# Mask factors by GpSimd, first loads in another order, and half of a layer's weights converted after attention

## The chip, the cores and the metric

The kernel runs on one core of one Trainium2 chip. The metric is device time in microseconds (us) of one execution. The core's engines are PE (matrix multiply; PEld is its weight load), DVE (vector), ACT (activations), POOL (GpSimd) and SP, which here issues every DMA. Each engine works through its own queue in order. A change of under 0.2%, about 2 us, can hardly be told from no change.

## What is computed

The inputs are the heads' `q`, `k`, `v` (4 sequences, 8 heads, 576 positions, 64 channels) and two layers' weights. Attention's mask is block-causal over blocks of 64 positions. The kernel receives every weight as 64-bit floats, which it reads as pairs of 32-bit words.

```python
scores = scale * q @ k.T            # (4, 8, 576, 576), masked: block_i >= block_j
attn   = softmax(scores)
x = (attn @ v) -> (2304, 512)
h = x @ w_in;  x = max(0.01*h, h) @ w_out                # first layer, 512 -> 2048 -> 512
h = x @ w_in2; g = P(h) / (Q(h) + 1e-6); out = g @ w_out2  # second layer, same shape
```

## The kernel before

**Stages.** The program runs 32 heads one after another (loop over `heads`). Behind the first batch of eight heads, the first layer of a finished batch is laid into the gaps: `moe1` is a generator that yields after each matmul, and `fill(n)` takes n of them between a head's steps. After the last head the rest of the first layer runs alone (32 calls of `fill(24)`, then `drain`): 512 tokens of the last batch, then 256 left-over tokens. Then `moe2`, the second layer, runs to the end. Matmuls take a number as a high and a low part (`wh`, `wl`), three products for one.

**Conversion.** `convert` is a generator that turns raw 64-bit weights into the two parts, block by block, two `yield`s (halves) for a block of 128 x 512 numbers. For each block SP loads 512 KB of raw words into a tile `cs` (three buffers, `load_block`). In the first half ACT scales the high words (line 165), and POOL (first nine blocks, line 169) or ACT (line 171) the low words. In the second half DVE joins them into `cl` (line 180), ACT rounds them to the high part (line 183), and POOL subtracts to get the low part (line 184). The first 32 blocks are the first layer's; their high part stays in SBUF and the low part is written to HBM (`w1l`). The last 32 blocks are the second layer's, two for each of 16 groups `f`; both parts are written to HBM (`w2h`, `w2l`, 256 KB each) and loaded again: groups 0 to 7 after attention, in the 32 `fill(24)` steps, into tiles `w2a` and into the space of the tiles `xh`, `xl` (`w2_in_x`), and groups 8 to 15 at the start of `moe2`.

**Order.** `pace` calls `cv` so that after head n `due[n]` halves are done: 65 up to head 14 (all of the first layer's blocks and one half) and 63 more over heads 15 to 31. Only SP's queue stands in the order of the code; a scheduler sets the other engines' orders from their dependences. Each DMA on SP's queue also waits for the landing of the one eight before it.

**Heads.** The first eight heads (`n < NSF`) multiply plain 32-bit tiles `fq`, `fk`: rows 0 to 63 hold q and k, rows 64 to 127 hold mask factors (`mask`: a memset, line 208, and an affine select, line 210, of 64 rows each, on POOL). There are four pairs of such tiles. POOL fills two pairs, and four DMAs copy the second pair's factors into pairs three and four (line 662). ACT scales q for each head (`a1`, line 243). In a head, scores go into PSUM tiles `T` of which four exist (`a2_part`, line 289 or 295), DVE takes maxima (line 301), ACT exponentiates (line 307), and the rows are divided by their sums (`a2_norm`, line 317, on DVE for the first eight heads and on POOL after). PE transposes the result (line 344), ACT and DVE move it out of PSUM (lines 327, 329, 334, 337), PE multiplies by v (lines 372, 376) and ACT and DVE take that out (lines 383 to 385, 389, 390, 393, 394; the last 64 positions go to HBM as `xld`).

Of the kernel before, what the change touches and what calls it, by code (L numbers as in the profile page):

```python
# [25 lines left out]
def attention_moe_moe_kernel(  # L26
# [13 lines left out]
    nc = tc.nc  # L40
# [78 lines left out]

    W1L = dram.tile([2 * NF, P, KD, P], F32, name="w1l")  # L120
    W2H = dram.tile([NF, P, 2 * KD, P], F32, name="w2h")
    W2L = dram.tile([NF, P, 2 * KD, P], F32, name="w2l")
# [4 lines left out]
    for g, c in enumerate(CUTS):  # L127
# [3 lines left out]
        for d in range(KD):  # L131
            src = w1_out[512 * g:512 * (g + 1), 2 * d * P:2 * (d + 1) * P].rearrange("(r p) w -> p r w", p=P)
            blocks.append((src, (w1o[:, 4 * g:4 * g + 4, d * P:(d + 1) * P], W1L[NF + 4 * g + d]), True))
    for f in range(NF):
        src = w2_in[:, 2 * f * P:2 * (f + 1) * P].rearrange("(r p) w -> p r w", p=P)
        blocks.append((src, (W2H[f, :, 0:KD, :], W2L[f, :, 0:KD, :]), False))
        src = w2_out[f * P:(f + 1) * P, :].rearrange("p (r w) -> p r w", r=KD)
        blocks.append((src, (W2H[f, :, KD:2 * KD, :], W2L[f, :, KD:2 * KD, :]), False))
    stage = {}
# [4 lines left out]
    def load_block(i):  # L144
        if i < len(blocks):
            stage[i] = cp.tile([P, 512, 2], I32, tag="cs", name="cs", bufs=3)
            nc.sync.dma_start(out=stage[i].rearrange("p (r n) w -> p r (n w)", r=KD), in_=blocks[i][0])

    split = []

# [6 lines left out]
    def convert():  # L157
        load_block(0)
        load_block(1)
        for i in range(len(blocks) + 1):  # L160
# [11 lines left out]
            if i > 0:  # L172
                s = stage.pop(i - 1)
                _, (dh, dl), kept = blocks[i - 1]
                hi, lo = s[:, :, 1], s[:, :, 0]
                f = cp.tile([P, KD, P], F32, tag="cl", name="cl", bufs=3)
                wh = dh if kept else cp.tile([P, KD, P], F32R, tag="ch", name="ch", bufs=2)
                hi, lo = (x.rearrange("p (r c) -> p r c", c=P) for x in (hi, lo))
                yield
                nc.vector.scalar_tensor_tensor(  # L180
                    f.bitcast(I32), hi, 3, lo, ALU.logical_shift_left, ALU.bitwise_or
                )
                nc.scalar.copy(wh, f)
                nc.gpsimd.tensor_tensor(f.bitcast(F32R), f, wh.bitcast(F32), ALU.subtract)
                write_block()
                split.append(((dh, wh.bitcast(F32)), (dl, f))[kept:])
                yield
        write_block()

    ndone = [0]  # L190
    conv = convert()

    def cv(n):
        for _ in range(n):
            next(conv, None)

    def cv_to(i):
        while ndone[0] < i:
            next(conv, None)

# [295 lines left out]
    def drain():  # L496
        while filler[0] is not None:
            fill(1000)


    chunks = [(NT1 * c, NT1) for c in range(B)] + [(B * NT1, B * NL)]
    W2 = {}

# [147 lines left out]
    with tc.manual_schedule(engines={mybir.EngineType.SP}):  # L651
        nc.scalar.preload_act_table_set("natural_log_exp_and_others")
        for n in range(4):
            load_qk(n)
        load_v(0)
        load_v(1)
        for c, (val, base) in enumerate(((1.0, 0), (NEG, 64))):
            mask(plain[0][c], val, base)
        for c, (val, base) in enumerate(((1.0, 0), (NEG, 64))):
            mask(plain[1][c], val, base)  # L660
            for j in (2, 3):
                nc.sync.dma_start(out=plain[j][c][D:P, :], in_=plain[1][c][D:P, :])
        make_identity(nc, ident)
        for e in range(2):
            for i in range(5):
                nc.gpsimd.memset(PB[e][i][:, KEYS[i]:], 0.0)
        nc.vector.memset(cq, 1.0 + EPS_Q)

        heads = [(b, h) for b in range(B) for h in range(H)]

        due = [0, 2, 4, 5, 9, 11, 13, 17, 22, 29, 36, 42, 48, 59, 65] + [65 + 63 * n // 17 for n in range(1, 18)]
        ncv = [0]
# [25 lines left out]
        for n, (b, h) in enumerate(heads):  # L698
# [8 lines left out]
            for step, f in zip(steps, fills):  # L707
                if step == "1" and n + 1 < NHD:
                    a1(n + 1)
                elif step == "v":  # L710
                    if n >= WHOLE:
                        a1v(n)
                    if n < WHOLE and odd and 0 < p:
                        load_v(p + 1)
# [38 lines left out]
        tiles = [w2_tiles(w2a, f) for f in range(NA)] + [w2_in_x(pair, f) for f in range(2)]  # L753
        loads = chain(*(load_w2_by_part(f, *t) for f, t in enumerate(tiles)))
        for i in range(32):
# [5 lines left out]
            elif i == 14:  # L761
                nc.scalar.copy(X[B][0], X[B][1].bitcast(F32))
                nc.vector.tensor_tensor(X[B][1], X[B][1].bitcast(F32), X[B][0].bitcast(F32), ALU.subtract)
                nc.vector.tensor_scalar(coef[:, 0:4], cab[:, 0:4], -1.0, None, ALU.mult)
                nc.scalar.activation(coef[:, 4:6], cab[:, 4:6], AF.Abs)
            elif i < 14:
                next(loads, None)
            elif i == 15:
                pair = x_tiles()
                loads = chain(*(load_w2_by_part(NA + 2 + f, *w2_in_x(pair, f)) for f in range(2)))  # L770
                loads = chain(loads, load_x2(0))
                filler[0] = moe1(B) if filler[0] is None else chain(filler[0], moe1(B))
            elif i % 2:
                next(loads, None)
        drain()
        store_x2()
# [43 lines left out]
```

## Time and profile before

| | us |
|---|---|
| median of 3 runs | 1042.35 (1041.92 to 1043.25) |
| the profiled execution | 1041.77 |
| its span, first to last instruction | 1040.0 |
| PE busy | 996.7 |
| DVE, ACT, POOL busy | 736.7, 668.9, 271.5 |

The profile is of one execution. The span is what the trace covers; 1.8 us of that execution lie outside it. PE's time is given as busy from a matmul's start to its modelled end, so matmuls in a row overlap, and what counts is where PE is idle.

### The profile page before, as it was taken

What the parts mean: (1) busy time and instruction counts of PE and PEld (TensorE: products, weight loads), DVE (VectorE), ACT (ScalarE), POOL (GpSimd) and SP (SyncE); (2) the same over time, 40 slices, a digit from 0 to 9 for tenths busy, and PEclk for the clock granted to TensorE, in tenths of its full rate; (3) what the DMA queues carried; (4) which work ended last, traced back from release to release, by engine and by line L of the source; (5) the groups of instructions that cost most, each with busy time, mean ns of one, the idle gap of its engine ahead of it and who ended that gap; (6) DMA issues with size and microseconds to landing.
All of it is one profiled execution on the core that took longest, in us unless ns stands there. A gap on an engine that the chain in (4) does not pass through costs nothing.

```text
span 1040.0 us, 14689 instructions
## 1 busy us (share of the span) xinstructions
PE 996.7 (96%) x4968; PEld 822.8 (79%) x4968; DVE 736.7 (71%) x1270; ACT 668.9 (64%) x1371; POOL 271.5 (26%) x325
## 2 busy tenths in 40 slices
PE   6989988999999989999999999999999999999998
PEld 4657776787888877888888899888888888888886
DVE  5897777676777767765322224999888888888885
ACT  5778878667776767675311324876766766676675
POOL 3366647464655544533100101000000000000000
PEclk9999999999999999999999999999999999999999
DMA  7467869468668676663755697702102000110010
GB/s 202 135 189 260 284 204 296 157 206 268 223 183 234 203 257 207 202 184 121 233 183 191 206 302 278 288 1 82 41 1 81 21 21 1 40 41 1 1 41 21
DMA packets 101995, 158.32 MB, mean 152 GB/s; under 512 B 11168, under 2 KB 48032, under 8 KB 101920
## 3 DMA queue, kind: packets, MB, share of 16 engines
q1 hardware_dynamic: 101920, 157.39, 47.4%
q8 instruction: 39, 0.64, 0.3%
q14 instruction: 36, 0.29, 0.1%
HBM read 116.92 MB, written 39.85 MB: 151 GB/s over the span
## 4 chain that ended last, share of the span: by engine, by line
PE 62%; DMA 11%; ACT 9%; DVE 8%; issue 4%; POOL 3%; SPq 2%; ACTq 0%; DVEq 0%; POOLq 0%
PE M L461 20%; PE h L563 19%; PE o L617 19%; DMA cs<-in_moe_w_in_dram 3%; ACT PB L307 3%; DVE nm L301 2%; DMA cs<-in_moe_w_out_dram 2%; DMA xld<-vr 2%; DVE cl L180 1%; ACT cs L165 1%; PE T L344 1%; ACT pTh L329 1%; PE T L376 1%; DMA qk<-in_k_dram 1%; DMA qk<-in_q_dram 1%
## 5 line engine op out<-in xcount | busy, mean ns | idle before, releaser
L461 PE MATMUL M<-gh,w1o 128*128 128x512 f32 (+1 forms) x320 | 121.3, 379 | 6.7 <-DVE vr L390 3.5
L461 PE MATMUL M<-gl,w1o 128*128 128x512 f32 (+1 forms) x320 | 120.7, 377 | 0.0
L461 PE MATMUL M<-gh,wl 128*128 128x512 f32 (+1 forms) x320 | 120.3, 376 | 0.0
L575 ACT ACTIVATE ea<-h,coef 128x512 f32<-128x512 f32 (+1 forms) x80 | 51.6, 645 | 92.7 <-PE h L563 92.7
L307 ACT ACTIVATE PB<-T,nm 128x448 f32<-128x448 f32 (+4 forms) x160 | 82.9, 524 | 36.1 <-DVE nm L301 35.0
L469 ACT ACTIVATE gh<-M 128x512 fp32r<-128x512 f32 (+1 forms) x80 | 44.5, 556 | 89.8 <-PE M L461 89.8
L471 DVE TENSOR_TENSOR gl<-M,gh 128x512 fp32r<-128x512 f32 (+1 forms) x80 | 50.6, 633 | 70.5 <-ACT M L470 70.5
L563 PE MATMUL h<-x2h,w2l 128*128 128x512 f32 (+1 forms) x240 | 88.9, 370 | 0.0
L563 PE MATMUL h<-x2h,w2h 128*128 128x512 f32 (+1 forms) x240 | 88.9, 370 | 0.0
L563 PE MATMUL h<-x2l,w2h 128*128 128x512 f32 (+1 forms) x240 | 88.8, 370 | 0.0
L617 PE MATMUL o<-w2h,g2l 128*128 128x512 f32 x216 | 84.7, 392 | 0.0
L617 PE MATMUL o<-w2h,g2h 128*128 128x512 f32 x216 | 84.7, 392 | 0.0
L317 POOL TENSOR_SCALAR PB<-PB,sm 128x448 f32<-128x448 f32 (+4 forms) x120 | 71.1, 612 | 51.9 <-DVE sm L314 51.9
L617 PE MATMUL o<-w2l,g2h 128*128 128x512 f32 x216 | 84.6, 391 | 0.0
L578 DVE SCALAR_TENSOR_TENSOR ea<-eh,coef,ea 128x512 f32<-128x512 f32 (+1 forms) x80 | 55.7, 696 | 34.9 <-ACT eh L576 34.5
L344 PE MATMUL T<-ident,PB 128*128 128x128 f32 x480 | 66.8, 278 | 11.5 <-ACT PB L307 4.8
L301 DVE TENSOR_REDUCE nm<-T 128x1 f32<-128x448 f32 (+4 forms) x160 | 71.3, 478 | 8.6 <-PE T L289 7.9
L461 PE MATMUL M<-xh,w1i 128*128 128x512 f32 x256 | 74.6, 401 | 2.8 <-DVE vr L390 2.5
L461 PEld LDWEIGHTS M<-gh,w1o 128*128 128x128 f32 x320 | 60.5, 189 | 19.0 <-ACT PB L307 3.9
L344 PEld LDWEIGHTS T<-ident,PB 128*128 128x128 f32 x480 | 54.6, 142 | 26.0 <-ACT PB L307 8.1
L180 DVE SCALAR_TENSOR_TENSOR cl<-cs 128x512 int32<-128x512 int32 x64 | 57.0, 892 | 23.0 <-ACT cs L171 9.6
L461 PE MATMUL M<-xh,wl 128*128 128x512 f32 x256 | 73.1, 401 | 0.0
(122 smaller groups left out, 2528.4 us busy)
## 6 DMA issues: line engine op xcount, KB each, us to landing
wl<-w1l SPq DMA_DIRECT2D x160, 256.0 KB, 3.3
cs<-in_moe_w_in_dram SPq DMA_DIRECT2D x32, 512.0 KB, 5.5
cs<-in_moe_w_out_dram SPq DMA_DIRECT2D x32, 512.0 KB, 5.7
w1l<-cl SPq DMA_DIRECT2D x32, 256.0 KB, 4.8
w2h<-ch SPq DMA_DIRECT2D x32, 256.0 KB, 4.1
w2l<-cl SPq DMA_DIRECT2D x32, 256.0 KB, 4.3
w2h<-w2h SPq DMA_DIRECT2D x12, 512.0 KB, 7.0
w2l<-w2l SPq DMA_DIRECT2D x12, 512.0 KB, 7.7
```

The source lines that it names most:

```text
L180: nc.vector.scalar_tensor_tensor(f.bitcast(I32), hi, 3, lo, ALU.logical_shift_left, ALU.bitwise_or)
L301: nc.vector.tensor_reduce(nm[:, i:i + 1], sc, axis=AX.X, op=ALU.max, negate=True)
L307: nc.scalar.activation(PB[e][i][:, 0:ln], sc, AF.Exp, scale=SCALE if n == 0 else 1.0, bias=nm[:, i:i + 1], accum_out=sm[:, i:i + 1])
L317: (nc.vector if n < WHOLE else nc.gpsimd).tensor_scalar(PB[e][i][:, 0:ln], PB[e][i][:, 0:ln], sm[:, i:i + 1], 1.0, ALU.mult, ALU.mult)
L344: nc.tensor.transpose(T[:, c:c + P], PB[e][i][:, kt * P:(kt + 1) * P], ident)
L461: nc.tensor.matmul(T, lhsT=w[:, kk, :], rhs=A[kk][lo], start=(m == 0), stop=(m == 11))
L469: nc.scalar.activation(gh, T, AF.Prelu, alpha=0.01)
L471: nc.vector.tensor_tensor(gl, T, gh.bitcast(F32), ALU.subtract)
L563: nc.tensor.matmul(h[:, 0:n], lhsT=a, rhs=x, start=(kk == 0 and i == 0), stop=(kk == KD - 1 and i == 2))
L575: nc.scalar.activation(a, h, AF.Abs, scale=coef[:, 4:5])
L578: nc.vector.scalar_tensor_tensor(a, h2, coef[:, 5:6], a, ALU.mult, ALU.add)
L617: nc.tensor.matmul(ob[t], lhsT=a, rhs=w, start=(f == 0 and i == 0), stop=(f == NF - 1 and i == 2))
```

## The change

There are three edits. First, POOL fills the mask factors of all four pairs (`masks(2)` and `masks(3)` after the identity and the memsets of `PB`), and the four copying DMAs go. Second, SP's first loads stand in another order: three heads' q and k, the first raw block (`cv_load`, which replaces the two loads at the head of `convert`), v of the first pair, the fourth head's q and k, the second raw block. The second pair's v, which was loaded at once, is now loaded behind head 1. Third, groups 8 to 15 of the second layer are converted first and as before. Groups 0 to 7 (`NRES` = 8, 16 blocks) are converted after attention, ACT and POOL writing straight into the tiles from which `moe2` reads; they are neither written to HBM nor loaded from there. `due` hands out 31 halves instead of 63 over heads 15 to 31, a limit (`halves`) stops `cv` at 96 halves in attention, and two halves go with each of the first 12 `fill(24)` steps and one with every second of the last 16.

```diff
-    for f in range(NF):
+    for f in chain(range(NRES, NF), range(NRES)):
...
-        blocks.append((src, (W2H[f, :, 0:KD, :], W2L[f, :, 0:KD, :]), False))
+        blocks.append((src, (W2H[f, :, 0:KD, :], W2L[f, :, 0:KD, :]) if f >= NRES else (f, 0), False))
...
+    first = iter((0, 1))
+    def cv_load():
+        load_block(next(first))
...
     def convert():
-        load_block(0)
-        load_block(1)
...
-                wh = dh if kept else cp.tile([P, KD, P], F32R, tag="ch", name="ch", bufs=2)
+                fl = f
+                if isinstance(dh, int):
+                    wh, fl = (
+                        x[:, 512 * dl:512 * (dl + 1)].rearrange("p (r c) -> p r c", c=P) for x in W2[dh]
+                    )
+                    kept = 2
+                else:
+                    wh = dh if kept else cp.tile([P, KD, P], F32R, tag="ch", name="ch", bufs=2)
...
-                nc.gpsimd.tensor_tensor(f.bitcast(F32R), f, wh.bitcast(F32), ALU.subtract)
+                nc.gpsimd.tensor_tensor(fl if kept == 2 else f.bitcast(F32R), f, wh.bitcast(F32), ALU.subtract)
                 write_block()
-                split.append(((dh, wh.bitcast(F32)), (dl, f))[kept:])
+                split.append(() if kept == 2 else ((dh, wh.bitcast(F32)), (dl, f))[kept:])
...
+    halves = [0, 2 * (2 * NF + 2 * (NF - NRES))]
...
-        for n in range(4):
+        for n in range(3):
             load_qk(n)
+        cv_load()
         load_v(0)
-        load_v(1)
-        for c, (val, base) in enumerate(((1.0, 0), (NEG, 64))):
-            mask(plain[0][c], val, base)
-        for c, (val, base) in enumerate(((1.0, 0), (NEG, 64))):
-            mask(plain[1][c], val, base)
-            for j in (2, 3):
-                nc.sync.dma_start(out=plain[j][c][D:P, :], in_=plain[1][c][D:P, :])
+        load_qk(3)
+        cv_load()
+        def masks(j):
+            for c, (val, base) in enumerate(((1.0, 0), (NEG, 64))):
+                mask(plain[j][c], val, base)
+        masks(0)
+        masks(1)
         make_identity(nc, ident)
...
+        masks(2)
+        masks(3)
...
-        due = [0, 2, 4, 5, 9, 11, 13, 17, 22, 29, 36, 42, 48, 59, 65] + [65 + 63 * n // 17 for n in range(1, 18)]
+        due = [0, 2, 4, 5, 9, 11, 13, 17, 22, 29, 36, 42, 48, 59, 65] + [65 + 31 * n // 17 for n in range(1, 18)]
...
-                    if n < WHOLE and odd and 0 < p:
+                    if n < WHOLE and odd:
                         load_v(p + 1)
...
-        loads = chain(*(load_w2_by_part(f, *t) for f, t in enumerate(tiles)))
+        W2.update(enumerate(tiles))
+        loads = iter(())
+        halves[1] = 4 * len(blocks)
...
-            elif i < 14:
-                next(loads, None)
             elif i == 15:
                 pair = x_tiles()
-                loads = chain(*(load_w2_by_part(NA + 2 + f, *w2_in_x(pair, f)) for f in range(2)))
-                loads = chain(loads, load_x2(0))
+                W2.update((NA + 2 + f, w2_in_x(pair, f)) for f in range(2))
+                loads = load_x2(0)
...
+            if i < 12:
+                cv(2)
+            elif i >= 16 and i % 2 == 0:
+                cv(1)
```

ACT's queue at the start, before. `fq_91`, `fq_93` and `fq_95` are q of heads 1, 2 and 3, `PB` and `T` of line 307 are head 0's exponentials.

```order
L243 ACTIVATE fq_91<-fq_91 64x576
L243 ACTIVATE fq_93<-fq_93 64x576
L243 ACTIVATE fq_95<-fq_95 64x576
L307 ACTIVATE PB_102,sm<-T,nm 128x448
L307 ACTIVATE PB_101,sm<-T,nm 128x320
```

The same place after the change (line 260 is the old 243, 324 the old 307, 172 the old 165).

```order
L260 ACTIVATE fq_91<-fq_91 64x576
L260 ACTIVATE fq_93<-fq_93 64x576
L172 ACTIVATE cs<-cs 128x512
L260 ACTIVATE fq_95<-fq_95 64x576
L324 ACTIVATE PB_102,sm<-T,nm 128x448
L324 ACTIVATE PB_101,sm<-T,nm 128x320
```

The first raw block's scaling now stands ahead of head 3's q and of head 0's exponentials.

SP's queue in the later part of attention, before, from one head's q and k to just before the next head's (`wl` is a low part for the first layer, `cs` a raw block, `w2h` and `w2l` writes of converted parts).

```order
L231 DMA qk_86<-in_q_dram 64x576
L232 DMA qk_86<-in_k_dram 64x576
L430 DMA wl<-w1l 128x512
L147 DMA cs<-in_moe_w_out_dram 128x1024
L154 DMA w2h<-ch 128x512
L154 DMA w2l<-cl 128x512
L430 DMA wl<-w1l 128x512
L237 DMA vr_87<-in_v_dram 128x4x128
L239 DMA vr_87<-in_v_dram 64x128 x2
L147 DMA cs<-in_moe_w_in_dram 128x4x256
L430 DMA wl<-w1l 128x512 x2
L154 DMA w2h<-ch 128x512
```

The same head after the change.

```order
L248 DMA qk_86<-in_q_dram 64x576
L249 DMA qk_86<-in_k_dram 64x576
L447 DMA wl<-w1l 128x512
L151 DMA cs<-in_moe_w_in_dram 128x4x256
L447 DMA wl<-w1l 128x512
L254 DMA vr_87<-in_v_dram 128x4x128
L256 DMA vr_87<-in_v_dram 64x128 x2
L447 DMA wl<-w1l 128x512 x2
L163 DMA w2h<-ch 128x512
L163 DMA w2l<-cl 128x512
```

One raw block and one pair of writes stand there instead of two.

ACT's queue after attention, in the stretch of the first layer alone, after the change (line 486 is the old 469, 487 the old 470; before, only such lines stood here). The tiles `w2h` belong to two groups `f`.

```order
L486 ACTIVATE gh<-M 128x512
L487 ACTIVATE M<-M 128x512
L172 ACTIVATE cs<-cs 128x512
L178 ACTIVATE cs<-cs 128x512
L197 CAST w2h_5007<-cl 128x512
L172 ACTIVATE cs<-cs 128x512
L178 ACTIVATE cs<-cs 128x512
L197 CAST w2h_5009<-cl 128x512
L172 ACTIVATE cs<-cs 128x512
L178 ACTIVATE cs<-cs 128x512
L197 CAST w2h_5009<-cl 128x512
L486 ACTIVATE gh<-M 128x512
```

Nine instructions of the conversion stand between two evacuations, where none stood.

## Rows read from the trace of the kernel before

**Rows 1.** The page: busy time, share of the span, instructions by engine.

```profile
PE 996.7 (96%) x4968; PEld 822.8 (79%) x4968; DVE 736.7 (71%) x1270; ACT 668.9 (64%) x1371; POOL 271.5 (26%) x325
```

**Rows 2.** By stretch: length, then PE, PEld, DVE, ACT, POOL busy, clock, DMA share, GB/s.

```profile
0.00:30.00 30.00, 19.03 (x82) 13.25 (x83) 16.67 (x41) 18.47 (x46) 10.69 (x30) 1.00 0.72 186
...
234.00:494.00 260.00, 250.35 (x1312) 207.85 (x1312) 180.95 (x313) 178.27 (x396) 127.41 (x152) 1.00 0.67 208
494.00:640.00 146.00, 146.00 (x818) 126.82 (x817) 40.74 (x72) 36.47 (x80) 13.24 (x12) 1.00 0.68 224
```

**Rows 3.** PE's waits, 234 to 494 us: who waited for whom, total us, times, longest.

```profile
PE M L461 <- DVE vr L390: 3.1, 5, 1.2
PE M L461 <- DVE xl L394: 1.5, 2, 1.2
PE T L295 <- DVE gl L471: 1.1, 1, 1.1
```

**Rows 4.** ACT's waits in the same stretch, same columns.

```profile
ACT ch L183 <- DMA w2h<-ch: 14.4, 7, 3.8
ACT cs L165 <- DMA cs<-in_moe_w_in_dram: 14.1, 7, 3.2
ACT cs L165 <- DMA cs<-in_moe_w_out_dram: 9.4, 5, 2.8
ACT vr L389 <- DMA xld<-vr: 5.2, 4, 2.6
```

**Rows 5.** Timeline, ACT and PE: start, length, instruction, idle before it and releaser.

```profile
243.42 0.67 ACT L165 ACTIVATE cs<-cs 128x512 f32<-128x512 f32 x1 [2.87 <-DMA cs<-in_moe_w_in_dram]
...
251.41 0.79 PE L295 MATMUL T<-split_fk,split_fq 128*128 128x288 f32 x4 [1.07 <-DVE gl L471]
```

**Rows 6.** Groups by line, 215 to 494 us: count, busy us, mean ns, idle before.

```profile
L184 POOL TENSOR_TENSOR cl<-cl,ch 128x512 fp32r<-128x512 f32 x30 | 43.0, 1433 | 55.8 <-ACT ch L183 50.1 <-DMA vr<-in_v_dram 3.9 <-DVE VHL L274 1.5
L180 DVE SCALAR_TENSOR_TENSOR cl<-cs 128x512 int32<-128x512 int32 x28 | 28.9, 1032 | 12.7 <-ACT cs L171 6.8 <-DMA w2l<-cl 5.7
L165 ACT ACTIVATE cs<-cs 128x512 f32<-128x512 f32 x28 | 19.1, 682 | 23.9 <-DMA cs<-in_moe_w_in_dram 14.3 <-DMA cs<-in_moe_w_out_dram 9.4
L171 ACT ACTIVATE cs<-cs 128x512 int32<-128x512 uint32 x28 | 18.8, 671 | 0.0
L183 ACT CAST ch<-cl 128x512 fp32r<-128x512 f32 x29 | 18.0, 621 | 14.7 <-DMA w2h<-ch 14.4
```

**Rows 7.** Timeline of the start, SP and ACT, columns as in rows 5.

```profile
4.56 0.60 SPq L231 DMA_DIRECT2D fq<-in_q_dram  x1
...
8.37 0.68 ACT L243 ACTIVATE fq<-fq 64x576 f32<-64x576 f32 x1 [1.03 <-DMA fq<-in_q_dram]
...
9.13 0.63 ACT L307 ACTIVATE PB<-T,nm 128x448 f32<-128x448 f32 x1
...
13.35 1.69 SPq L147 DMA_DIRECT2D cs<-in_moe_w_in_dram  x3
...
18.53 0.65 ACT L165 ACTIVATE cs<-cs 128x512 f32<-128x512 f32 x1 [1.18 <-DMA cs<-in_moe_w_in_dram]
18.59 0.64 POOL L169 TENSOR_SCALAR cs<-cs 128x512 int32<-128x512 uint32 x1 [12.64 <-DMA cs<-in_moe_w_in_dram]
```

**Rows 8.** Timeline of the start, PE and what it waits for.

```profile
13.21 1.56 DVE L317 TENSOR_SCALAR PB<-PB,sm 128x448 f32<-128x448 f32 x5
...
13.80 0.30 PE L344 MATMUL T<-ident,PB 128*128 128x128 f32 x1 [1.82 <-DVE PB L317]
...
20.03 1.56 PE L289 MATMUL T<-fk,fq 128*128 128x448 f32 x4 [1.78 <-ACT acc L327]
...
22.33 4.05 DVE L317 TENSOR_SCALAR PB<-PB,sm 128x448 f32<-128x448 f32 x5
...
23.39 2.58 POOL L184 TENSOR_TENSOR cl<-cl,w1i 128x512 fp32r<-128x512 f32 x2
...
26.14 0.95 PE L344 MATMUL T<-ident,PB 128*128 128x128 f32 x5 [0.95 <-DVE PB L317]
```

More of the change, by code (lines that the diff above doesn't have):

```diff
@@ L120, in attention_moe_moe_kernel @@
     W1L = dram.tile([2 * NF, P, KD, P], F32, name="w1l")
+    NRES = 8
     W2H = dram.tile([NF, P, 2 * KD, P], F32, name="w2h")
@@ L133, in attention_moe_moe_kernel @@
             blocks.append((src, (w1o[:, 4 * g:4 * g + 4, d * P:(d + 1) * P], W1L[NF + 4 * g + d]), True))
-    for f in range(NF):
+    for f in chain(range(NRES, NF), range(NRES)):
         src = w2_in[:, 2 * f * P:2 * (f + 1) * P].rearrange("(r p) w -> p r w", p=P)
-        blocks.append((src, (W2H[f, :, 0:KD, :], W2L[f, :, 0:KD, :]), False))
+        blocks.append((src, (W2H[f, :, 0:KD, :], W2L[f, :, 0:KD, :]) if f >= NRES else (f, 0), False))
         src = w2_out[f * P:(f + 1) * P, :].rearrange("p (r w) -> p r w", r=KD)
-        blocks.append((src, (W2H[f, :, KD:2 * KD, :], W2L[f, :, KD:2 * KD, :]), False))
+        blocks.append((src, (W2H[f, :, KD:2 * KD, :], W2L[f, :, KD:2 * KD, :]) if f >= NRES else (f, 1), False))
+    W2 = {}
     stage = {}
@@ L194, in cv @@
         for _ in range(n):
-            next(conv, None)
+            if halves[0] < halves[1]:
+                halves[0] += 1
+                next(conv, None)
     def cv_to(i):
         while ndone[0] < i:
-            next(conv, None)
+            cv(1)
     def vi(p):
@@ L501, in attention_moe_moe_kernel @@
     chunks = [(NT1 * c, NT1) for c in range(B)] + [(B * NT1, B * NL)]
-    W2 = {}
     NA = 4
@@ L774, in attention_moe_moe_kernel @@
                 next(loads, None)
+            if i < 12:
+                cv(2)
+            elif i >= 16 and i % 2 == 0:
+                cv(1)
         drain()
```

## The prediction

> **What bounds the kernel now.** I read the engines' busy shares first: PE is busy 996.7 of 1040.0 us, the next engine, DVE, 736.7 [rows 1]. So time can only come from PE's idle stretches, and the second view, the table by stretch, says where they are [rows 2]. After attention (494 to 640 us) PE is busy for the whole 146.00 us, and ACT for only 36.47. In attention PE idles 10.97 us of the first 30 and 9.65 us from 234 to 494. Between, up to about 234 us, the change hands out the conversions head by head as before; from there to 494 it hands out half. Third, I looked at who keeps PE waiting between 234 and 494: DVE's `vr`, `xl` and `gl` [rows 3]. None of these is a conversion, so the fourth view asks what delays the engines that feed them. ACT waits there for DMAs of the conversion: 14.4 us until a written `w2h` has left its buffer, 14.1 and 9.4 us for raw blocks, and 5.2 us more for the small `xld` write that stands behind them in the same queue [rows 4]. ACT works in order, so an evacuation that stands behind such a wait is late. One place shows it [rows 5]: ACT stands idle for 2.87 us before 243.42, for a raw block, and PE then waits 1.07 us for `gl` at 251.41. The wait for `xld` stands before the ACT copy of `vr`, on which DVE's `vr` rests.
>
> **Conversions that leave attention.** Sixteen of 32 second-layer blocks go. By the mean of each line [rows 6] ACT loses 16 x (0.682 + 0.671 + 0.621) = 31.6 us, DVE 16 x 1.032 = 16.5 us and POOL 16 x 1.433 = 22.9 us between 234 and 494; SP loses 16 loads of 512 KB and 32 writes of 256 KB, 16.8 MB of the 54.1 MB that 208 GB/s in 260 us make [rows 2]. None of this work is on PE's path by itself; what it can return is PE's 9.65 us of idle time there. The lower bound is nothing, if all the idle time is attention's own chain. The upper bound is the 9.65 us; a loss has no place, since SP, ACT, DVE and POOL only lose work in that stretch, except by a less lucky order, for which I allow 1 us. I choose 5.0 us: half the conversions mean half the places where ACT can be caught, each wait also gets shorter in a queue that carries a third less, and the PE waits for `vr`, `xl` and `gl`, 5.7 us [rows 3], are those that stand behind ACT. The rest I leave to the ends of batches, where PE waits for the last head whatever ACT does.
>
> **The same conversions after attention.** The 31.6 us of ACT, 16.5 of DVE and 22.9 of POOL now lie between 494 and 640: ACT comes to 68 us of 146, DVE to 57, POOL to 36 [rows 2, 6]. On the queues 16 raw loads of 512 KB take the place of 16 loads of 512 KB of converted parts, so DMA carries what it carried, and the write of the last block, which stood between the two layers, goes. I cost this at nothing. What hides it is that PE has four PSUM tiles and its evacuations leave ACT idle for 110 of 146 us. If that cover is gone, the price is a PE wait in each of the 12 `fill` steps that carry a block: nine ACT instructions of the conversion can stand ahead of an evacuation, 3 x 1.97 = 5.9 us, while one unit of twelve matmuls lasts at most 3 us (146 us hold 32 long and 32 half-long units, 48 long ones, and the end of attention). The order puts those nine where four `out` units, some 11 us, run, which need no ACT at all; so 0, with 0 to 8 us as the range.
>
> **The start.** Head 3's q was the seventh DMA, issued at 4.56, and ACT took it at 8.37, 3.8 us later [rows 7]. Now it is the eleventh: at 0.64 us an issue it goes out at 4.56 + 4 x 0.64 = 7.1, and 512 KB of raw block and v of a pair stand ahead of it. The nearest row for a raw block says 5.2 us from issue to use (13.35 to 18.53) [rows 7], so the one issued seventh, at 4.56, is usable at 9.8. Head 3's q follows between 7.1 + 3.8 = 10.9 and some 12.5, I take 11.6. In ACT's queue the first raw block and that q now stand ahead of head 0's first exponential, which ran at 9.13: it moves to 11.6 + 0.7 = 12.3, later by 3.2 us, and with it PE's first transposes, from 13.80 to about 17.0 [rows 8]. What comes back: at 20.03 PE waited 1.78 us for an ACT copy that stood behind a raw block, for which ACT had waited 1.18 us and then worked 0.65 [rows 7, 8]. That block is now done by 12, so PE, which has 2.4 us of transposes and 1.2 us of scores to do from 17.0, gets there at 20.5: late by 0.4 us. Next, head 1's division took DVE 4.05 us, where head 0's took 1.56, with two subtractions of POOL running from 23.39 to 25.97, and PE waited 0.95 us for it at 26.14 [rows 8]. In the new order the first subtraction stands well ahead of that division and the next ones further apart, so I expect one to meet it and not two: a gain of 1.3 us on DVE, and with the waits just before it 1.7 us on PE. Net gain of the start: 1.3 us, between a loss of 3.2 (nothing comes back) and a gain of 3.
>
> On that collision the Trainium skill, page SBUF — State Buffer, section "Who interferes with whom", says that DVE and GpSimd share a pair of ports as an exclusive lock and the later one stands for the whole instruction. By that rule each subtraction that starts first costs the division its 1.3 us, so one fewer would return 1.3 us and none at all 2.6; the trace's 4.05 against 1.56 us agrees. The page DMA: Bandwidth & Descriptors, section "Queues, rings and completion order", says that descriptors of a ring are taken in order, by which head 3's q could not pass the raw block; if it could, it would land at 10.9 and the start would gain 0.7 us more.
>
> The mask factors: four more memsets and four selects on POOL, about 4 us, lie behind the identity, where POOL was idle for 12.64 us before its first conversion [rows 7]; they are done near 10, as the first raw block lands. Head 2's scores need them, at about 19 in the new order. Cost nothing; without that cover they would hold the first conversion by up to 4 us. Four DMAs less on SP save 2.4 us of issue ahead of head 4's loads, which wait for head 0's scores anyway. The second pair's v is wanted only after the second scores of head 2 (20.03 [rows 8]) and goes out near 12.
>
> **Sum.** Against the profiled execution: 1041.77 - 5.0 - 0 - 1.3 = 1035.5. The median of the runs is 0.58 above that execution, so the forecast is 1036.1.
>
> **Rivals.**
> A. Attention's own chain holds PE, not the conversions. PE's waits in rows 3 name DVE, and DVE has 181 us of work in 260. Then the later heads return 1 us and the start, losing as much as it wins back, nothing: 1042.35 - 1 = 1041.3. Against it speak 43 us of ACT waits for DMAs in that stretch.
> B. All of the idle time there goes and the start gains 3: 1042.35 - 9.65 - 3 = 1029.7. Against it: batch ends remain.
> C. Slower: conversions hold PE after attention. ACT comes to a raw block that has not landed, as it did in 12 cases of attention for 23.5 us together, 2.0 us each [rows 4], with evacuations behind it. It decides once ACT's wait and the conversion's three instructions, 2.0 + 2.0 us, exceed what the PSUM tiles and the one unit between a group's last `in` unit and its use allow, some 3 + 1 us by the unit length above. If each of the 16 blocks then cost 1 us, and the start loses its 3.2 us: 1042.35 - 5 + 16 + 3.2 = 1056.6; with half of it 1047. For it: the rows show such waits. Against: loads after attention are one for every two units, and DMA is no busier there than in attention, 0.68 against 0.67 [rows 2].
> D. The start's delay stays: 3.2 us lost in place of 1.3 won, 1036.1 + 4.5 = 1040.6.
>
> **How the numbers follow.** The forecast, 1031 to 1040, has a chance of 0.65; A 0.12, B 0.07, C 0.08, D 0.08. Half of D counts as the same. Faster by over 0.2% (below 1040.3): 0.65 + 0.07 + 0.04 = 0.76. Within 0.2%, which is about what a measurement can tell from nothing: 0.12 + 0.04 = 0.16. Slower: 0.08. For 8 in 10 the range takes the forecast and D and the nearer part of A: 1031 to 1041.2, which leaves out B, C and the rest of A.
>
> **What would show it.** If right, PE's idle time from about 234 us to the end of attention falls from 9.65 to about 5 us, ACT's DMA waits there from 43 us to under 20, the stretch after attention stays at a full PE, and head 0's first exponential starts near 12.3 us with PE at 20.5 for head 2's second scores. Wrong would be: PE waits between 494 and 640 (C), ACT's DMA waits gone but PE's idle time kept (A), or the whole of attention shifted by the 3 us of the start (D).

## The result and the profile after

The changed kernel takes 1033.39 us (median of 4 runs, 1031.29 to 1035.20), the kernel before, run beside it, 1042.13 (4 runs). The ratio is 0.9916, with a 95% interval of 0.9891 to 0.9941: faster by 8.7 us, where the forecast was 6.2 against the runs shown then (1036.1 against 1042.35). The profiled execution took 1033.04 us with a span of 1031.3. Line numbers of after are up to 17 higher than those of before.

The table by stretch, columns as in [rows 2]:

```profile
0.00:30.00 30.00, 20.24 (x81) 14.60 (x81) 17.60 (x41) 19.05 (x46) 16.59 (x40) 0.94 0.63 160
...
234.00:494.00 260.00, 256.50 (x1354) 218.13 (x1353) 170.38 (x302) 161.84 (x363) 110.97 (x141) 0.99 0.53 161
494.00:640.00 146.00, 144.79 (x810) 125.62 (x810) 53.64 (x92) 67.09 (x132) 28.84 (x25) 1.00 0.69 228
```

PE's idle time from 234 to 494 falls from 9.65 to 3.50 us (4.85 in a second trace of the same kernel, below), and in this trace it no longer waits there for DVE's `vr` and `gl` [rows 3]. PE's waits of after, 225 to 482 us, where attention ends (who waited for whom, total us, times, longest):

```profile
PE T L361 <- ACT PB L324: 2.2, 2, 2.1
PE M L478 <- ACT xh L410: 1.0, 1, 1.0
PE M L478 <- DVE xl L411: 0.9, 1, 0.9
PE T L389 <- ACT pTh L346: 0.3, 1, 0.3
```

Four points in the traces divide the gain: the last matmul of attention ends at 492.8 us before and at 481.8 after, the second layer starts at 636.9 and 627.9. The division of head 15 (DVE's reciprocal of its sums) lies at 210.9 and 210.3.

| stretch | before | after | difference | forecast |
|---|---|---|---|---|
| to head 15's division | 210.9 | 210.3 | -0.6 | -1.3 |
| from there to attention's last matmul | 281.8 | 271.5 | -10.3 | -5.0 |
| first layer alone | 144.1 | 146.1 | +2.0 | 0 |
| second layer | 403.1 | 403.3 | +0.2 | 0 |

So the sign and the place were right, and the three sizes were not. One trace divides no finer than some us: from head 15's division to attention's last matmul the same kernel took 272.8 us in its second trace, and 275.6 in a kernel (below) that differs from it only after attention. The experiments ask first which edit pays, then what in the moved conversions had held PE.

### The profile page after: what moved, and what is told of

Read it like the earlier page. It is cut to its first block, busy times and chain, and to the rows that moved or that the text cites. A ratio compares the mean times of both kernels' runs of the same rounds, so it can differ in the third digit from the quotient of the medians.

```text
span 1031.3 us, 14580 instructions
## 1 busy us (share of the span) xinstructions
PE 994.9 (96%) x4968; PEld 827.7 (80%) x4968; DVE 734.0 (71%) x1270; ACT 672.0 (65%) x1371; POOL 271.9 (26%) x333
## 4 chain that ended last, share of the span: by engine, by line
PE 76%; DMA 6%; ACT 6%; DVE 5%; issue 3%; POOL 2%; SPq 1%; ACTq 0%; DVEq 0%; POOLq 0%
PE M L478 28%; PE h L579 19%; PE o L633 19%; PE T L361 3%; PE T L393 3%; PE T L312 2%; ACT PB L324 2%; DMA w1l<-cl 2%; DMA cs<-in_moe_w_in_dram 2%; ACT cs L172 1%; DVE nm L318 1%; DMA fq<-in_q_dram 1%; PE T L306 1%; DVE PB L334 1%; DMA wl<-w1l 1%
## 5 line engine op out<-in xcount | busy, mean ns | idle before, releaser
L172 ACT ACTIVATE cs<-cs 128x512 f32<-128x512 f32 x64 | 43.2, 676 | 50.6 <-DMA cs<-in_moe_w_in_dram 29.6
L361 PEld LDWEIGHTS T<-ident,PB 128*128 128x128 f32 x480 | 57.0, 144 | 22.3 <-issue 5.6
```

Source lines behind the costliest of these rows:

```text
L172: nc.scalar.activation(hi.bitcast(F32), hi.bitcast(F32), AF.Prelu, scale=2.0 ** -112, alpha=-(2.0 ** 32))
L361: nc.tensor.transpose(T[:, c:c + P], PB[e][i][:, kt * P:(kt + 1) * P], ident)
```

## Which edit pays: each alone

The third edit alone, with the old start (edits are against after):

```diff
-        for n in range(3):
+        for n in range(4):
             load_qk(n)
-        cv_load()
         load_v(0)
...
-        masks(2)
-        masks(3)
```

> The kernel before with the third edit alone: 16 blocks converted after attention, the start as before. Theory A (the thinned conversions make all but 0.5 us of the gain; the two traces show head 0's division 3.0 us late, head 4 to 15 about 0.5 us early, and the last 16 heads 10 us earlier): 1033.5 to 1035.5, head 15 at the time of before within 0.5 us, last attention matmul 9 to 10 us earlier than before. Theory B (the start's order puts every later conversion a step ahead and that is what frees the later heads): 1037 or more.

Measured: 1033.74 us (6 runs) beside 1041.52 (18 runs), ratio 0.9929 [0.9906, 0.9952]: 7.8 us faster. In its trace, of an execution 3 us above that median, attention's last matmul ends 6.3 us earlier than before, where 9 to 10 was expected.

The first two edits alone, with all conversions where they were before:

```diff
-        due = [0, 2, 4, 5, 9, 11, 13, 17, 22, 29, 36, 42, 48, 59, 65] + [65 + 31 * n // 17 for n in range(1, 18)]
+        due = [0, 2, 4, 5, 9, 11, 13, 17, 22, 29, 36, 42, 48, 59, 65] + [65 + 63 * n // 17 for n in range(1, 18)]
...
-    for f in chain(range(NRES, NF), range(NRES)):
+    for f in range(NF):
```

> The kernel before with the first two edits alone: mask factors by POOL and the new order of first loads; all 32 blocks converted in attention. Theory A: 1041 to 1042, that is within 1 us of before, with head 0's division near 15.7 us instead of 12.7 and the delay gone by head 4. Theory B: 1038 or less. My forecast's own term: 1040.8.

Measured: 1041.66 us (12 runs), ratio 1.0005 [0.9986, 1.0024]. The start alone is worth nothing that can be measured. In its trace head 0's sums are divided at 16.95 us, and head 4's at 51.2 are still 2.6 us late, where the delay was expected to be gone. After itself was run once more on the same chip:

> The changed kernel as it is, on the same chip as the three others, to compare them with: 1031 to 1035, with its spread.

It took 1033.24 us (7 runs), ratio 0.9921 [0.9892, 0.9950]. The third edit's 7.8 us are thus nearly all of the 8.3.

## What the start gives and takes

The timeline of after's start shows the delay that was forecast, and what came back (columns as in rows 5):

```profile
9.21 0.68 ACT L172 ACTIVATE cs<-cs 128x512 f32<-128x512 f32 x1 [1.91 <-DMA cs<-in_moe_w_in_dram]
11.67 0.68 ACT L260 ACTIVATE fq<-fq 64x576 f32<-64x576 f32 x1 [1.78 <-DMA fq<-in_q_dram]
12.26 0.61 ACT L324 ACTIVATE PB<-T,nm 128x448 f32<-128x448 f32 x1
...
13.52 1.56 PE L306 MATMUL T<-fk,fq 128*128 128x448 f32 x4 [2.62 <-ACT PB L324]
...
16.18 2.97 DVE L334 TENSOR_SCALAR PB<-PB,sm 128x448 f32<-128x448 f32 x5
...
16.73 1.45 POOL L198 TENSOR_TENSOR cl<-cl,w1i 128x512 fp32r<-128x512 f32 x1 [1.48 <-ACT w1i L197]
16.77 0.30 PE L361 MATMUL T<-ident,PB 128*128 128x128 f32 x1 [1.69 <-ACT w1i L197]
...
22.00 1.27 POOL L198 TENSOR_TENSOR cl<-cl,w1i 128x512 fp32r<-128x512 f32 x1 [3.02 <-ACT w1i L197]
22.02 1.27 DVE L330 TENSOR_SCALAR sm<-sm 128x5 f32<-128x5 f32 x1
...
24.10 1.57 DVE L334 TENSOR_SCALAR PB<-PB,sm 128x448 f32<-128x448 f32 x5
```

ACT takes the fourth head's q at 11.67 (forecast 11.6), head 0's first exponential starts at 12.26 (forecast 12.3, before 9.13) and PE's transposes at 16.77 (forecast 17.0). That the exponential came to the tenth is luck: in the ten traces of this document with that order of loads it starts at 12.03 to 13.59, and in after's second trace at 13.59. What was to come back did not come where it was forecast: PE reaches head 2's second scores at 23.01, where 20.5 was forecast and 20.03 stood before. Head 0's sums are divided 3.0 us later than before, head 1's 2.2, head 2's 1.3, head 3's 0.3, and head 4's 0.5 us earlier (0.5 us later in the second trace).

The division of head 1 lost its 4.05 us [rows 8]: it takes 1.57, with no subtraction of POOL beside it. But head 0's, which took 1.56, now meets one and takes 2.97, and so does the step ahead of head 1's division, which adds a constant to its sums (line 330). It takes 1.27 us beside a subtraction of the same length; before, it took 0.17:

```profile
21.04 0.17 DVE L313 TENSOR_SCALAR sm<-sm 128x5 f32<-128x5 f32 x1 [0.40 <-ACT PB L307]
```

So the collision moved, and on the first two heads DVE won nothing by it: these four steps take 1.56 + 4.05 + 0.17 + 0.17 = 5.95 us before and 2.97 + 1.57 + 0.37 + 1.27 = 6.18 after. The divisions of heads 2 and 3 are the ones that come free, with 1.57 us each, from 2.58 and 1.96, and there the delay shrinks.

One price of the late exponential was in no term of the sum. In the trace with the start alone, PE waits 3.78 us for it, and the clock falls (table by stretch, then the timeline):

```profile
0.00:30.00 30.00, 18.98 (x67) 13.48 (x68) 16.28 (x36) 16.67 (x40) 15.60 (x39) 0.83 0.62 160
```

```profile
14.07 2.31 PE L292 MATMUL T<-fk,fq 128*128 128x448 f32 x4 [3.78 <-ACT PB L310]
```

The mean granted clock of these 30 us is 0.83, against 1.00 before [rows 2] and 0.94 in after's trace: PE had stood idle, and for part of the stretch it was then granted 1.2 in place of 2.4 GHz. In after's trace that part lies just ahead of head 2's second scores:

```profile
19.40:22.80 3.40, 3.40 (x14) 2.97 (x14) 2.67 (x6) 2.89 (x8) 0.80 (x1) 0.51 0.89 260
```

To see whether the delay itself has a price, the fourth head's q was put ahead of the raw block again, with the rest of after kept:

```diff
-        for n in range(3):
+        for n in range(4):
             load_qk(n)
         cv_load()
         load_v(0)
-        load_qk(3)
         cv_load()
```

> The changed kernel with head 3's q and k loaded ahead of the first raw block and of v, as before the change; nothing else moved. If the 3 us by which head 0's division is late come from that load, that division returns from 15.7 to between 12.7 and 13.5 us. If those 3 us are only lent (ACT has as much conversion to do either way and head 4 comes when it did): head 4 at 48 us and the whole within 1 us of the changed kernel. If they are lost for good, head 4 at about 45.5 us and the whole 2 to 3 us faster than the changed kernel, 1030 to 1031.

```profile
10.23 0.65 ACT L172 ACTIVATE cs<-cs 128x512 f32<-128x512 f32 x1 [1.32 <-DMA cs<-in_moe_w_in_dram]
10.78 0.62 ACT L324 ACTIVATE PB<-T,nm 128x448 f32<-128x448 f32 x1
```

The exponential starts at 10.78 and not near 9.1, since the scaling of the raw block, for which ACT waits 1.32 us, still stands ahead of it in ACT's queue. Head 0's sums are divided at 14.3 us, not by 13.5, and head 4's at 47.2 (after 48.2, and 49.2 in its second trace), the first 30 us run at a clock of 1.00, and the time is 1032.01 us (6 runs), ratio 0.9906 [0.9888, 0.9924]. The median is 1.2 us below after's beside it; the two intervals overlap, so that gain is not shown.

## What held PE in late attention: work or transfers

The prediction's reason was that ACT, waiting for the conversion's DMAs, comes late to its evacuations. ACT's waits for DMAs in after, up to the end of attention:

```profile
ACT cs L172 <- DMA cs<-in_moe_w_in_dram: 12.6, 6, 5.3
ACT cs L172 <- DMA cs<-in_moe_w_out_dram: 10.4, 5, 3.2
ACT ch L197 <- DMA w2h<-ch: 7.9, 5, 3.2
...
ACT vr L406 <- DMA xld<-vr: 3.7, 3, 1.4
```

They are 34.6 us, from 43.1 [rows 4], where "under 20" was forecast; and yet PE's idle time fell to 3.50 (in the second trace 36.9 us of such waits go with 4.85 of idle time). A fall of a fifth in the supposed cause does not go with a fall of two thirds in the effect. The other reading is that the instructions themselves cost, whether or not they wait. Three kernels put the 16 blocks back into heads 15 to 31, beside the 16 that are there, each with a part of what a block is. `MORE` marks them. The conversion after attention stays as it is in after. The extra results are dropped, or written where nothing reads them. In the rows of these kernels and of the later ones that put work back, line numbers are 10 to 24 higher than after's.

```diff
-    for f in chain(range(NRES, NF), range(NRES)):
+    for f in [g for e in range(NRES) for g in (NRES + e, -1 - e)] + list(range(NRES)):
+        if f < 0:
+            f = -1 - f
+            for o in (0, 1):
...
+                blocks.append((src, (W2H[f, :, o * KD:(o + 1) * KD, :], W2L[f, :, o * KD:(o + 1) * KD, :]), MORE))
+            continue
...
-        due = [0, 2, 4, 5, 9, 11, 13, 17, 22, 29, 36, 42, 48, 59, 65] + [65 + 31 * n // 17 for n in range(1, 18)]
+        due = [0, 2, 4, 5, 9, 11, 13, 17, 22, 29, 36, 42, 48, 59, 65] + [65 + 63 * n // 17 for n in range(1, 18)]
```

**Transfers alone**: the raw loads and the writes of the 16 blocks, with no instruction of ACT, DVE or POOL (the writes take a tile that is already there).

> The changed kernel, and in heads 15 to 31 the DMAs of the 16 removed blocks come back with no engine work: the 512 KB of raw words are loaded into a buffer and not used, and two writes of 256 KB go out from a tile that no longer changes. 11 us of attention (its last matmul at 492.8 before, 482 after) are in question. Theory D (ACT's waits for DMAs made the stalls): most comes back, last attention matmul at 489 or later, time 1039 to 1042. Theory W (the engines' own work made them): at most 2 us come back, 482 to 484, time 1033 to 1035.

**Work alone**: the five instructions of a block, reading a weight tile in SBUF, with no load and no write.

> The changed kernel, and in heads 15 to 31 the engine work of the 16 removed blocks comes back with no DMA: ACT's three, DVE's one and POOL's one instruction for each on old data in SBUF, result dropped. Theory D: at most 3 us come back, last attention matmul by 485, time 1033 to 1036. Theory W: 489 or later, 1039 to 1042.

**Loads and work**, without the writes.

> The changed kernel, and in heads 15 to 31 the 16 removed blocks come back with raw loads and engine work but without their writes, result dropped. If the wait for a buffer whose write has not landed (14.4 us of ACT's waits before, 7.9 after) is what counts, attention ends at 486 or earlier; if loads and work count together, 489 to 493 and 1039 to 1043.

| kernel | median us (runs) | before beside it | ratio (95%) | attention's last matmul |
|---|---|---|---|---|
| after | 1033.39 (4) | 1042.13 (4) | 0.9916 [0.9891, 0.9941] | 481.8 |
| transfers back | 1039.32 (12) | 1043.49 (23) | 0.9975 [0.9951, 0.9998] | 488.9 |
| work back | 1043.55 (12) | 1043.49 (23) | 0.9999 [0.9981, 1.0017] | 494.4 |
| loads and work back | 1052.24 (6) | 1043.49 (23) | 1.0085 [1.0060, 1.0111] | 502.5 |

These kernels, and those of the next section, are not after with a part added and nothing else changed. The 16 blocks that are there come in pairs (in the first two kernels 22 to 32 us from one pair to the next), where after scales one every 13 to 23 us. And the scheduler set each order anew: from head 15's division to attention's last matmul, 1 to 8 of ACT's 260 other instructions and 4 to 11 of DVE's 310 stand elsewhere than in after (1 and 3 in the kernel before). What these shifts cost by themselves was not tried.

Work back, from the table by stretch, then PE's waits and ACT's, both from 225 to 494 us:

```profile
234.00:494.00 260.00, 249.28 (x1310) 208.13 (x1311) 186.35 (x315) 179.99 (x397) 123.29 (x153) 1.00 0.50 153
```

```profile
PE T L378 <- ACT PB L341: 4.2, 7, 1.2
PE M L495 <- DVE vr L424: 4.0, 2, 2.9
PE M L495 <- DVE xl L428: 2.0, 2, 1.2
```

```profile
ACT ch L214 <- DMA w2h<-ch: 7.2, 4, 3.4
ACT cs L189 <- DMA cs<-in_moe_w_out_dram: 4.4, 3, 2.6
ACT vr L423 <- DMA xld<-vr: 2.7, 2, 2.0
ACT cs L189 <- DMA cs<-in_moe_w_in_dram: 2.2, 4, 0.9
```

ACT's waits for DMAs are only 16.5 us here, half of after's, and DMA is at 0.50 of its time. Yet PE idles 10.72 us and the whole gain is gone, more than was expected for it. The prediction's sentence that "none of this work is on PE's path by itself" is not borne out: the work takes the gain back with no transfer of its own. One place of this kernel shows how work and a wait add up:

```profile
230.14 0.68 ACT L189 ACTIVATE cs<-cs 128x512 f32<-128x512 f32 x1 [1.41 <-DMA cs<-in_moe_w_out_dram]
...
232.49 0.62 ACT L214 CAST ch<-cl 128x512 fp32r<-128x512 f32 x1 [0.60 <-DVE cl L211]
233.13 0.63 ACT L423 COPY vr<-T 64x576 f32<-64x576 f32 x1
...
233.79 0.75 DVE L424 TENSOR_TENSOR vr<-T,vr 64x576 f32<-64x576 f32 x1 [0.74 <-ACT vr L423]
...
234.60 1.15 PE L495 MATMUL M<-xh,w1i 128*128 128x512 f32 x3 [2.90 <-DVE vr L424]
```

ACT's copy of `vr`, for which PE stands still, has to follow a whole block of the conversion: its scalings, for which ACT waited 1.41 us (this block is one that after has there too), and its rounding, which waited for DVE's second join in a row. DVE then comes, and PE has lost 2.90 us.

But transfers are not free either. With them alone (table by stretch, PE's waits, ACT's wait for `xld`, 225 to 494 us):

```profile
234.00:494.00 260.00, 253.92 (x1331) 213.81 (x1331) 172.23 (x305) 159.06 (x359) 102.94 (x138) 0.99 0.71 214
```

```profile
PE M L496 <- DVE vr L425: 4.9, 4, 2.5
PE M L496 <- DVE xl L429: 1.9, 2, 1.0
```

```profile
ACT vr L424 <- DMA xld<-vr: 8.4, 6, 2.6
```

Half of the gain is gone, 1043.49 - 1039.32 = 4.2 us being left, and PE's waits for `vr` are back. Which wait carries it is not shown. ACT's copy of `vr` now waits 8.4 us for the small `xld` write, from 3.7, and behind the longest of these, 2.57 us until 351.32, PE waits 0.57 us; but ACT's waits for DMAs together come to 31.9 us, less than after's 34.6. PE's longest wait for `vr`, 2.51 us at 232.15, stands behind two scalings and a rounding of a block and an ACT wait of 2.38 us for POOL. One more place is as the prediction has it: ACT waits 4.95 us for a raw block until 300.68, and PE then 0.62 us for `vr` at 303.47. The costs do not add up: of the 8.5 us that after gains (8.7 and 8.3 in its two comparisons), work takes back 8.6 and transfers 4.3. Loads and work without writes were worse than before, which neither theory expected; ACT waits 19.1 us there for `w_out` blocks, and why that pairing is the worst was not settled.

## Which engine's work

Three kernels put back the work of one engine alone, all without transfers, in the same place of the order: ACT's three instructions for each of the 16 blocks, DVE's one, POOL's one.

```diff
+                if kept == MORE:
+                    nc.gpsimd.tensor_tensor(f.bitcast(F32R), w, w2, ALU.subtract)
```

(DVE: the join of two words, ACT: two scalings and a copy, in its place.)

> The changed kernel, and in heads 15 to 31 only ACT's three instructions of each of the 16 removed blocks come back, on old data in SBUF, result dropped; no DMA, no DVE, no POOL. With all engines' work back attention ended at 494.4 us, 12.6 later than with the change (481.8). Theory A (ACT, which stands between PE and PSUM, is what the conversions held up): 6 us or more come back, last attention matmul at 488 or later, 1038 to 1042. Theory P (POOL's subtractions, which delay the divisions and hold DVE, did it): 484 or earlier, 1033 to 1035.

> The same with DVE's one instruction of each of the 16 blocks alone, 16.5 us of DVE time. DVE takes the maxima and half of the evacuations, so I expect 2 to 4 us back, last attention matmul at 484 to 486; under both theories it is the smaller part.

> The same with POOL's one subtraction of each of the 16 blocks alone, 22.9 us of POOL time. Theory A: at most 2 us back, last attention matmul by 484, 1033 to 1035. Theory P: 6 us or more, 488 or later, 1038 to 1042. If the three engines' parts add up to about 12.6 us the work counts as a sum; if they come to much less, it is their chain.

| put back | its work in the trace, us | median us (12 runs each) | ratio to 1041.54 (29 runs) | given back of 8.5 | attention's last matmul, later by |
|---|---|---|---|---|---|
| ACT | 31.2 | 1037.93 | 0.9965 [0.9948, 0.9982] | 4.9 | 7.2 |
| DVE | 13.6 | 1039.95 | 0.9988 [0.9970, 1.0007] | 6.9 | 5.4 |
| POOL | 21.8 | 1037.24 | 0.9957 [0.9939, 0.9975] | 4.2 | 4.1 |

Late attention by stretch, with ACT's work, with DVE's, with POOL's:

```profile
234.00:494.00 260.00, 254.17 (x1335) 214.35 (x1336) 173.06 (x306) 182.20 (x402) 104.92 (x140) 0.99 0.52 155
```

```profile
234.00:494.00 260.00, 253.99 (x1338) 214.25 (x1337) 179.03 (x315) 158.33 (x357) 106.48 (x139) 1.00 0.52 157
```

```profile
234.00:494.00 260.00, 254.21 (x1341) 214.22 (x1342) 174.86 (x303) 159.25 (x358) 120.37 (x152) 1.00 0.53 158
```

There is no one guilty engine: PE idles 5.8 to 6.0 us with any of the three, where after has 3.5 and before 9.65. From head 15's division to attention's last matmul it idles 7.2, 8.6 and 8.8 us, where before has 10.7 and the five traces with after's late attention 4.4 to 6.8. The three together would give back 16 us by their medians, and all the work together gave back 8.6, so they overlap; that the others' lateness costs less where one engine is late already would explain it, and was not shown. POOL's part, which touches no evacuation, still costs 4 us; POOL also divides the rows of these heads, and ACT's copy of `vr` waits 3.9 us for its divisions there, 0.6 in after. DVE's part, for which 2 to 4 us were expected as the smaller part, has the highest cost of the three. PE waits for `vr` in all three (3.8 to 4.1 us). Of ACT's 7.2 us by the trace, some 2 had been lost before head 15, in a start in which the clock was at 0.83; its median is the better number. The intervals are about 2 us wide on either side, so the order of the three is not settled.

## The end of attention, and both mends together

After attention PE loses a little, where nothing was forecast and none of its waits stood before. PE's waits of after, 482 to 629 us:

```profile
PE h L579 <- DVE acc L495: 0.5, 1, 0.5
PE M L478 <- DMA wl<-w1l: 0.4, 1, 0.4
PE M L478 <- DVE acc L495: 0.3, 1, 0.3
```

The wait for `wl` suggests the loads of the second layer's first inputs, which in after go out in the steps from 17 on, since nothing stands ahead of them in `loads` any more. They were put back to steps 25 and 27:

```diff
-            elif i % 2:
+            elif i % 2 and i >= 25:
                 next(loads, None)
```

> The changed kernel with the second layer's first input loaded in steps 25 and 27 of the last stretch, as before the change, and not in 17 and 19. In that stretch PE now waits 0.56 us for a low part of weights at 594.6, behind 2 MB of these loads, and the stretch is 2.0 us longer than before. If the loads make that: the wait goes and the stretch is 145.5 us or shorter instead of 146.1; the rest of the 2.0 us stays. If the conversions make it all, nothing changes. Time within 1 us of the changed kernel either way.

The waits in that stretch shrink to one:

```profile
PE h L579 <- DVE acc L495: 0.5, 1, 0.5
```

The first layer alone takes 144.8 us (146.1 in after, 144.1 before): 1.3 of the 2.0 us were these loads. It takes 144.8 in the next kernel too, which has this edit, and 145.1 to 146.3 in the ten traces with the third edit and the early loads. The median, 1035.22 us (6 runs) with a ratio of 0.9921 [0.9898, 0.9944], doesn't show so small a gain. Last, this edit and the fourth head's q ahead of the raw block together:

> The changed kernel with head 3's q and k ahead of the first raw block and with the second layer's first input loaded in steps 25 and 27. The first made head 4 come 1 us earlier and the median 1.2 us lower (both within the spread), the second took 1.3 us off the stretch after attention. If both hold: 1030.5 to 1032.5, stretch after attention 145 us or shorter. If the start's gain is only lent: 1032 to 1034.

It took 1030.53 us (6 runs) beside 1041.54, ratio 0.9893 [0.9865, 0.9921]: 11.0 us faster than the kernel before, and the best of all that ran. Head 4 is divided at 46.6 us, the first layer alone takes 144.8, and in its trace the clock stays at 1.00 up to the last matmuls:

```profile
0.00:30.00 30.00, 20.30 (x88) 14.20 (x89) 18.43 (x45) 20.80 (x51) 17.03 (x40) 1.00 0.67 170
...
234.00:494.00 260.00, 255.30 (x1351) 216.68 (x1352) 169.78 (x302) 161.52 (x363) 111.72 (x142) 1.00 0.52 160
494.00:640.00 146.00, 145.48 (x816) 126.45 (x815) 55.47 (x95) 68.46 (x135) 28.14 (x24) 1.00 0.71 232
```

That it beats after itself is likely and not shown: the intervals of the two ratios overlap.

## Why the prediction was right, and where it was not

**What bounds the kernel.** Right: the gain lies in late attention, where PE's idle time was, whatever the change does elsewhere.

**Conversions that leave attention.** This is the term that was mis-sized: 5.0 us forecast, 10.3 in the profiled execution, 6.2 to 10.3 in the five traces with after's late attention, and 7.8 in the medians of the third edit alone. Two steps of it failed. First, the reason: ACT's waits for DMAs were taken for the cause, and the work for harmless. Put back alone, each takes back some of the gain, the work more by the medians; so the count of ACT's waits, 34.6 us instead of "under 20", foretold nothing. Second, the 9.65 us of idle time were taken for all that can come back. Of the idle time itself the forecast was near, since 3.50 us are left (3.9 to 4.9 in the four other traces) where "about 5" was named; what came on top shows in no idle time (below). What is left is not only the ends of batches, where PE waits "whatever ACT does": in after these are 0.86 us at 232.6, just ahead of the stretch, and 0.99 at 365.7. One place makes 2.06, and the prediction's own mechanism is seen in it:

```profile
235.58 0.65 ACT L172 ACTIVATE cs<-cs 128x512 f32<-128x512 f32 x1 [5.30 <-DMA cs<-in_moe_w_in_dram]
...
237.23 1.33 PE L361 MATMUL T<-ident,PB 128*128 128x128 f32 x8 [2.06 <-ACT PB L324]
```

ACT stands 5.30 us for a raw block, the exponentials behind it are late, and PE waits 2.06 us. That PE gained more than its idle time fell (10.3 against 6.2) has two parts. Three matmuls, 0.5 us from start to start, run before head 15's division in after and behind it in before. And idle time is not all that PE loses: from each matmul's start to the next one's, against the median for its shape, PE lost 24.3 us in late attention before and 14.4 after (14.4 to 18.4 in the five traces). A matmul of the first layer is 0.39 us long by its modelled end, and the next one mostly starts 0.23 us behind it, so one that comes up to 0.16 us late shows no idle time. So 9.65 us was no upper bound.

**The same conversions after attention.** 0 forecast, +2.0 measured, of which 1.3 come from a load that the change lets out early; the prediction followed `w2`'s loads through that queue and not the ones behind them. ACT's 67.09 and DVE's 53.64 us of work from 494 to 640 are near what was worked out (68 and 57; POOL's 28.84 less than the 36), and the cover held: the rival in which the conversions hold PE there is out.

**The start.** The delay was forecast rightly (12.3 us for the first exponential, 12.03 to 13.59 in ten traces). What was to bring it back was not: PE came to head 2's second scores at 23.01 instead of 20.5, and heads 0 and 1 had no gain from the subtractions. The net is 0 in the medians, and at head 4 0.5 us won in one trace of after and 0.5 lost in the other, against 1.3. What the sum lacked is the subtractions that now meet head 0's division and head 1's sums, and the lower clock behind PE's longer wait. On that collision the rule of the Trainium skill, page SBUF — State Buffer, section "Who interferes with whom", is borne out once more: 1.57 us without a subtraction beside the division, 2.97 with one, and head 1's step, which came 0.02 us behind its subtraction, ended with it.

**The masks** were done at 9.71 us, and POOL began its first conversion at 9.80: nothing lost that shows. They were not tried alone.

The errors were on both sides: 5.3 us too little in late attention, 0.7 and 2.0 too much in the start and the end. That the sum came within 2.7 us is in part luck. The rival nearest in size to what happened in late attention is B, all of the idle time returned, which had the least chance of all.

**Left open**: why loads with work are worse than before; how the parts' 16 us shrink to 8.6 in detail; by which wait the transfers cost; how much of each cost comes from the changed order and places of the other instructions; and whether the start, which alone is worth nothing, is worth something beside the third edit (attention ended at 486.4 us in the trace with the third edit alone, and at 481.1 to 483.4 in the five with both or most of the new start, but that execution was 3 us above its kernel's median).

## What to carry to other kernels

An engine that works in order between PE and its PSUM tiles can be on PE's path at two thirds load already (ACT was busy for 178 of 260 us here, DVE for 181): instructions put into its queue, or into the queue of an engine that feeds it, cost a share of their length even with no transfer of their own. Here 14 to 31 us of work on one engine cost the kernel 4 to 7. To judge such a move, don't add up the engine's waits, but put the work back without its transfers, and the transfers without the work; and don't expect the parts to add up. If a stretch without such evacuation pressure exists, as the first layer alone was here, background work belongs there.

## What the hardware showed unasked

A short idle time of PE can cost more than itself, and does not always. Behind the wait of 2.06 us at 237.23, after's table by stretch reads:

```profile
232.00:237.00 5.00, 2.55 (x10) 1.80 (x10) 1.50 (x3) 1.40 (x4) 0.02 (x1) 1.00 0.99 270
237.90:241.30 3.40, 3.40 (x13) 2.57 (x12) 1.37 (x3) 3.40 (x9) 0.00 (x0) 0.50 0.98 322
241.30:246.00 4.70, 4.70 (x26) 4.02 (x25) 4.18 (x8) 2.33 (x5) 3.26 (x4) 1.00 0.22 58
```

PE is busy for 2.55 of 5.00 us, then runs 3.4 us at a granted clock of 0.50, which is 1.2 GHz, and is back at 2.4 GHz with 26 matmuls in the next 4.7 us, where 13 went into the 3.4. After's second trace has a wait of 1.84 us at the same place, the best kernel one of 2.01 and the kernel with the work back one of 2.90, and there the clock stays at 1.00, so the wait alone does not decide it. At the start it divides the kernels: in all ten traces with the fourth head's q behind the raw block PE waits 2.4 to 4.7 us for head 0's exponentials and is granted the lower level for 3.4 to 10.2 us, from about the end of that wait or up to 6 us behind it. In the four with that q ahead of it (before, the third edit alone, and the two mended ones) no wait of PE behind its first scores is longer than 2.1 us, and it keeps 2.4 GHz through the first 30 us.
